# MoE 2 in program order: one queue of weight pieces, pairs and single units in turn, and second products moved into the next unit

## The chip, the cores and the metric

One core of one Trainium2 chip. The metric is the device time of one execution in microseconds (us). Engines: PE (TensorE) multiplies, ACT (ScalarE) copies and applies relu, DVE (VectorE) subtracts, POOL (GpSimd) issues the indirect transfers, SP (SyncE) issues the others.

## The reference

Attention (4 batches, 8 heads, 512 local tokens with a window of 32 to each side, 32 global tokens) gives 2176 rows of 512. Two layers follow:

```
h = x @ w_in                      # 2176x512 @ 512x2048
x = maximum(0.01 * h, h) @ w_out  # MoE 1
logits = normed(x) @ normed(expert_emb).T / tau      # 8 experts
e = argmax(logits); gate = softmax(logits)[e]        # one expert for each token
out = gate * (maximum(x @ w1[e], 0) @ w2[e])         # MoE 2, 512 -> 1024 -> 512
```

All of it is float32. A product is made of three: each operand is split into a high part (rounded to the format PE takes) and a low part (the rest), and PE adds high*high, high*low and low*high.

## The kernel before

The rows are worked on in tiles of 128. Attention is interleaved with MoE 1, which runs over blocks of tiles and, in each, 16 steps of `L1` (first product) and `L2` (second). When 14 of the 17 tiles are done, `make_plan(0)` plans units 0 to 2 of MoE 2; the last three tiles are routed later (`Q0` to `Q4`), and `make_plan(1)`, `make_plan(2)` plan the rest, on DVE, in pieces spread over unit 1.

A **unit** is a group of tokens of one expert. Units 0 to 7 are pairs (two blocks of 128 tokens): eight steps f, each with a first product `D1(u, f)` and, one step later, the second product `D2(u, f)`; between them ACT makes the relu's high part (`g`, L972) and DVE its low part (L973). Units 8 to 13 are singles (one block): `M1(u, j)` for two halves j, relu into `hs` (ACT for j = 0, DVE for j = 1), transposes `HT` on PE into `tp`, `ht` high by ACT (L927) and low by DVE (L928), second product `M2(u, j)`. `ORDER` is the order of the units: 0, 1, 2, 3, 8, 4, 9, 5, 10, 6, 11, 12, 13, 7. More units follow only if the plan needs them.

A unit's weights (4 MB) come by `load_w`, two conditional transfers from SP, into one of two buffers ("lanes": `w1a`, `w2a` and `w1b`, `w2b`); the transfer is skipped where the lane holds that expert already. They are then split in eight **pieces**, a cast on ACT (L863) and a subtraction on DVE (L864) each, for the next unit while this one runs. The tokens' numbers come by `load_ids` (SP, from `idl`, the list that the routing scatters in memory by POOL, L634), their rows by `gather` (POOL, `xg`), and `X2` transposes them (PE L898, ACT `xgT` L899, DVE `xgl` L900). `out_rows` scales (ACT `yo`, L936) and scatters (POOL, L937).

PE and SP run MoE 2 in the order in which the code is written, DVE in units 0 and 1 alone; elsewhere, and on ACT throughout, a scheduler of the framework sets the order. Half of unit 0's pieces are made in the last steps of MoE 1, the others behind its end. At the end of unit 2 the code waits for lane 0 to be free (`load_w(3)`), then loads unit 8 into lane 1, then reads the ids of units 3, 4, 5 and of the singles.

Of the kernel before, what the change touches and what calls it, by code (L numbers as in the profile page):

```python
# [24 lines left out]
def kernel(  # L25
# [519 lines left out]
    def Q0(q, yp):  # L545
# [7 lines left out]
        if NTILE - NL + q == NTILE - 1:  # L553
            x2 = sb.tile([P, XW], F32, tag="xs", bufs=2, name="x2")
# [65 lines left out]
    def Q4():  # L620
# [6 lines left out]
        V.tensor_copy(si, ss[:, 4])  # L627
        V.tensor_reduce(out=ss[:, 5], in_=lg, axis=AX.X, op=ALU.add)
# [107 lines left out]
    def make_plan(phase):  # L736
# [132 lines left out]
    def pieces_w1(u, j):  # L869
        w = w1s[u, j] = sb.tile([P, 2, KM, DM], F32R, tag="half", bufs=8, name="w1s")  # L870
        return split(w, lanes[lane_of[u]][0][:, :, j * DM:(j + 1) * DM])

    def pieces_w2(u, j):
        w = w2s[u, j] = sb.tile([P, 2, 4, DM], F32R, tag="half", bufs=8, name="w2s")
        return split(w, lanes[lane_of[u]][1][:, 4 * j:4 * j + 4, :])
# [29 lines left out]
    def M1(u, j):  # L905
        xT = xts[u]
        w = w1s.pop((u, j))
        hp_ = ps.tile([P, DM], F32, tag="H", name="hp2")
        for a, c in ((0, 0), (1, 0), (0, 1)):
            for k in range(KM):  # L910
                nc.tensor.matmul(
                    hp_, xT[a][:, k, :], w[:, c, k, :], start=(a + c + k == 0), stop=(c == 1 and k == KM - 1)
                )
        hs = sb.tile([P, DM], F32, tag="g", bufs=2, name="hs")
# [27 lines left out]
    def M2(u, j, part):  # L942
        w, ht = w2s[u, j], hts[u, j]
        if j == part == 0:
            ys[u] = ps.tile([P, DM], F32, tag=ybank[u], name="yp2")
        yp = ys[u]
        todo = [(a, c, f) for a, c in ((0, 0), (1, 0), (0, 1)) for f in range(4)]
        for a, c, f in todo[6 * part:6 * part + 6]:
            nc.tensor.matmul(  # L949
                yp, ht[:, a, f, :], w[:, c, f, :], start=(j + a + c + f == 0), stop=(j == c == 1 and f == 3)  # L950
            )
        if part == 0:
            return
        w2s.pop((u, j))
        hts.pop((u, j))
# [4 lines left out]
    def D1(u, f):  # L960
        w = w1s[u, f // 4]
# [7 lines left out]
        if f % 4 == 3:  # L969
            w1s.pop((u, f // 4))  # L970
# [133 lines left out]
    while k < len(steps):  # L1104
        i, f = steps[k]
        if k == KF * (2 * B - 1) + 6:
# [4 lines left out]
            load_w(0)  # L1111
# [33 lines left out]
        if k >= KF * (2 * B - 1) + 10:  # L1145
            if k == KF * (2 * B - 1) + 10:
                lanes[1] = (
                    sb.tile([P, KM, F2], F32, tag="half", bufs=8, name="w1b"),
                    sb.tile([P, KF2, DM], F32, tag="half", bufs=8, name="w2b"),
                )  # L1150
# [3 lines left out]
            first = first[1:]  # L1154
# [26 lines left out]
    def planned(n):  # L1181
        for _ in range(n):
            next(plan_pieces, None)

    pend = []

    def behind():
        if pend:
            pend.pop(0)()

    def unit(k):
# [3 lines left out]
        rest_ = pieces(after) if after is not None else iter(())  # L1195
        same = [m for m in range(k + 1, len(ORDER)) if LANE[m] == LANE[k]]
        if same:
            load_w(ORDER[same[0]])
        if k == NDE - 1:
            load_w(ORDER[LANE.index(1)])  # L1200
# [110 lines left out]
```

## Time and profile before

| | |
|---|---|
| median of 3 runs | 939.44 us (937.65 to 941.67) |
| the profiled execution's own time | 941.09 us |
| its span, first to last instruction | 939.4 us |
| mean granted clock of PE, share of full speed | 0.963 |
| PE busy | 863.3 us, 92% of the span |
| DVE, ACT, POOL busy | 545.5 (58%), 491.5 (52%), 161.1 (17%) |

Own time is what the device takes for the execution; the span is what the profiler saw between its first and last instruction. A busy PE is one with a product under way, at whichever clock.

### The profile page before, as it was taken

Reading aid. Unit: us, or ns where it says so; the run is one execution under the profiler, and the core shown is the slowest. Engines: PE = TensorE matmul, PEld = TensorE weight load, DVE = VectorE, ACT = ScalarE, POOL = GpSimd, SP = SyncE. Lnnn points to the kernel's source line nnn. Section 1 sums busy time; section 2 is a strip of 40 time slices with the busy share of each in tenths; the row PEclk is TensorE's granted clock in tenths of the full one; section 3 lists DMA queues with packets and bytes.
Section 4 is the critical chain, followed back from the end, with each engine's and each line's share of the span. In section 5 each row is a group of like instructions: output and inputs, shape, how many; then the busy total and the mean of one; then the engine's idle time right before and its main releaser. Section 6 shows DMA issues by size and latency. Waiting matters only on the chain.

```text
span 939.4 us, 16083 instructions
## 1 busy us (share of the span) xinstructions
PE 863.3 (92%) x5852; PEld 735.0 (78%) x5852; DVE 545.5 (58%) x1397; ACT 491.5 (52%) x1181; POOL 161.1 (17%) x218
## 2 busy tenths in 40 slices
PE   6768699999999999999999999989796999999996
PEld 3646587888888888888888888978685877878785
DVE  6788898344654554555534345455763566665850
ACT  6877787444645544545423232471452566565841
POOL 3532443001100100000001000210203031220200
PEclk9697899999999999999999999989997999999999
DMA  9676553110121210110000001600157566277600
GB/s 229 168 201 165 148 170 87 44 45 13 36 46 43 54 44 12 46 29 1 12 13 12 12 12 17 220 23 1 45 198 262 202 231 218 87 259 262 229 14 17
DMA packets 104551, 92.21 MB, mean 98 GB/s; under 512 B 73415, under 2 KB 81735, under 8 KB 104466
## 3 DMA queue, kind: packets, MB, share of 16 engines
q1 hardware_dynamic: 98002, 78.51, 27.4%
q0 software_dynamic: 4064, 10.25, 3.4%
q10 hardware_dynamic: 2400, 2.36, 0.8%
q8 instruction: 48, 0.79, 0.4%
q14 instruction: 37, 0.30, 0.1%
HBM read 97.56 MB, written 11.63 MB: 116 GB/s over the span
## 4 chain that ended last, share of the span: by engine, by line
PE 69%; DVE 9%; DMA 8%; issue 6%; ACT 6%; POOL 1%; SPq 1%; POOLq 0%; ACTq 0%; DVEq 0%
PE hps L681 20%; PE yp L703 7%; PE hps L966 7%; PE yp L984 6%; PE yp L705 6%; PE yp L704 6%; DMA out_dram<-yo,ids 2%; DMA ids<-idl 2%; PE av L254 2%; PE pp L240 2%; PE sp L203 2%; PE ga L315 2%; PE yp L949 2%; ACT pr L224 1%; PE lp L505 1%
## 5 line engine op out<-in xcount | busy, mean ns | idle before, releaser
L688 ACT COPY gf<-hps 128x256 f32<-128x256 f32 (+1 forms) x144 | 50.3, 361 | 177.0 <-PE hps L681 176.1
L689 DVE SCALAR_TENSOR_TENSOR gf<-gf 128x256 f32<-128x256 f32 (+1 forms) x144 | 60.0, 425 | 135.6 <-ACT gf L688 135.2
L703 PE MATMUL yp<-woh,g 128*128 128x512 f32 x272 | 114.5, 421 | 0.7 <-ACT g L691 0.7
L984 PE MATMUL yp<-w2s,g 128*128 128x512 f32 x384 | 104.7, 407 | 9.0 <-DVE g L973 6.5
L705 PE MATMUL yp<-woh,g 128*128 128x512 f32 x272 | 107.8, 396 | 1.5 <-DVE g L692 1.5
L704 PE MATMUL yp<-wol,g 128*128 128x512 f32 x272 | 107.5, 395 | 0.0
L984 PEld LDWEIGHTS yp<-w2s,g 128*128 128x128 f32 x384 | 69.1, 194 | 24.6 <-DVE g L973 10.2
L692 DVE TENSOR_TENSOR g<-gf,g 128x256 fp32r<-128x256 f32 (+1 forms) x144 | 60.8, 431 | 42.9 <-ACT g L691 37.4
L966 PE MATMUL hps<-xgT,w1s 128*128 128x256 f32 x512 | 84.3, 288 | 0.0
L966 PEld LDWEIGHTS hps<-xgT,w1s 128*128 128x128 f32 x512 | 75.0, 194 | 4.8
L681 PE MATMUL hps<-xs,wih 128*128 128x256 f32 x448 | 75.6, 291 | 3.2 <-ACT gf L688 3.2
L691 ACT CAST g<-gf 128x256 fp32r<-128x256 f32 (+1 forms) x144 | 55.3, 395 | 34.4 <-DVE gf L689 34.2
L681 PEld LDWEIGHTS hps<-xs,wih 128*128 128x128 f32 x448 | 65.1, 190 | 9.5 <-ACT gf L688 3.4
L681 PE MATMUL hps<-xs,wil 128*128 128x256 f32 x448 | 71.2, 281 | 0.0
L681 PE MATMUL hps<-xl,wih 128*128 128x256 f32 x448 | 71.2, 281 | 0.0
L972 ACT ACTIVATE g<-hps 128x256 fp32r<-128x256 f32 x64 | 24.5, 382 | 86.3 <-PE hps L966 84.3
L705 PEld LDWEIGHTS yp<-woh,g 128*128 128x128 f32 x272 | 51.2, 188 | 14.5 <-DVE g L692 2.4
L703 PEld LDWEIGHTS yp<-woh,g 128*128 128x128 f32 x272 | 51.2, 188 | 12.6 <-issue 4.1
L681 PEld LDWEIGHTS hps<-xs,wil 128*128 128x128 f32 x448 | 60.9, 189 | 0.0
L681 PEld LDWEIGHTS hps<-xl,wih 128*128 128x128 f32 x448 | 60.9, 189 | 0.0
L704 PEld LDWEIGHTS yp<-wol,g 128*128 128x128 f32 x272 | 51.4, 189 | 6.4
L973 DVE SCALAR_TENSOR_TENSOR g<-hps,g 128x256 fp32r<-128x256 f32 x64 | 26.9, 420 | 50.6 <-ACT g L972 50.6
(273 smaller groups left out, 1768.6 us busy)
## 6 DMA issues: line engine op xcount, KB each, us to landing
w1a<-in_moe_w_dram SPq DMA_DIRECT2D x9, 2048.0 KB, 8.4
w2a<-in_moe_w_dram SPq DMA_DIRECT2D x9, 2048.0 KB, 10.8
w1b<-in_moe_w_dram SPq DMA_DIRECT2D x5, 2048.0 KB, 7.8
w2b<-in_moe_w_dram SPq DMA_DIRECT2D x5, 2048.0 KB, 10.1
raw<-in_moe_w_in_dram SPq DMA_DIRECT2D x14, 512.0 KB, 3.7
raw<-in_moe_w_out_dram SPq DMA_DIRECT2D x14, 512.0 KB, 4.6
x2d<-x SPq DMA_DIRECT2D x16, 256.5 KB, 2.8
kn<-in_k_l_dram SPq DMA_DIRECT2D x31, 128.0 KB, 2.8
```

Of the source, the lines that this page charges most:

```text
L681: nc.tensor.matmul(hps, ws[a][:, k], xs[c][k], start=(a + c + k == 0), stop=((a, c) == (1, 0) and k == KM - 1))
L688: nc.scalar.copy(gf, hps[:, cs])
L689: nc.vector.scalar_tensor_tensor(out=gf, in0=gf, scalar=0.01, in1=gf, op0=ALU.mult, op1=ALU.max)
L691: nc.scalar.copy(g[:, 0], gf)
L692: nc.vector.tensor_tensor(out=g[:, 1], in0=gf, in1=g[:, 0].bitcast(F32), op=ALU.subtract)
L703: nc.tensor.matmul(yp, g[:, 0], hi, start=(f == 0), stop=False)
L704: nc.tensor.matmul(yp, g[:, 0], lo, start=False, stop=False)
L705: nc.tensor.matmul(yp, g[:, 1], hi, start=False, stop=(f == KF - 1))
L966: nc.tensor.matmul(hps, w[:, a, k, fs], xts[u][c][:, k], start=(a + c + k == 0), stop=(a == 1 and k == KM - 1))
L972: nc.scalar.activation(out=g[:, 0], in_=hps, func=AF.Relu)
L973: nc.vector.scalar_tensor_tensor(out=g[:, 1], in0=hps, scalar=0.0, in1=g[:, 0].bitcast(F32), op0=ALU.max, op1=ALU.subtract)
L984: nc.tensor.matmul(ys[u, t], g[:, a, t * P:(t + 1) * P], w[:, c, f % 4, :], start=(f + a + c == 0), stop=(f == KF2 - 1 and a == 1),)
```

## The change

MoE 2 is rewritten so that DVE, SP and ACT, beside PE, run it in the order of the code. Pairs use lane 0, singles lane 1; `ORDER` becomes 0, 1, 2, 8, 3, 9, 4, 10, 5, 11, 6, 12, 7, 13. All eight pieces of unit 0 are made in the last six steps of MoE 1. All other pieces stand in one list, `todo`, taken one at each step of units 0 to 2, (2, 2, 1, 2, 1, 2, 1, 1) in a later pair, 2 + 2 in a single; a lane's next load is issued as soon as the lane's last piece is out. The squares of `Q0` become `Q0S` and stand in unit 0's first three steps; the routing and the planning end earlier (`Q4` at step 5 of unit 0, planning from its step 7 to step 3 of unit 1), and `plan_end` follows at step 4 of unit 1, with the weights and the ids of unit 8 first. A single's two second products stand behind the first two steps of the next pair, and a pair's last second product, in two halves, behind the two first products of the single that follows. The numbers of products, pieces and conditional loads are as before (PE has 4 instructions fewer).

```diff
+        rt[q, "x2"] = x2
+
+    def Q0S(q):
         sq = sb.tile([P, DM], F32, tag="x2T", bufs=2, name="sq")
-        nc.scalar.activation(out=sq, in_=x2[:, 0:DM], func=AF.Square, accum_out=lt_["sl3"][:, 0, q:q + 1])
-        rt[q, "x2"] = x2
+        nc.scalar.activation(
+            out=sq, in_=rt[q, "x2"][:, 0:DM], func=AF.Square, accum_out=lt_["sl3"][:, 0, q:q + 1]
+        )
...
-    ORDER = [0, 1, 2, 3, 8, 4, 9, 5, 10, 6, 11, 12, 13, 7]
-    LANE = [0, 0, 0, 0, 1, 0, 1, 0, 1, 0, 1, 0, 1, 0]
-    lane_of = dict(zip(ORDER, LANE))
-    for u in range(ND + NS, NUNIT):
-        lane_of[u] = u % 2
+    ORDER = list(range(NDE))
+    for i in range(max(NS, ND - NDE)):
+        ORDER += ([ND + i] if i < NS else []) + ([NDE + i] if NDE + i < ND else [])
+    lane_of = {u: 0 if u < ND else 1 for u in range(NUNIT)}
...
-    def pieces(u):
-        for j in range(2):
-            for make in (pieces_w1, pieces_w2):
-                for piece in make(u, j):
-                    piece()
-                    yield
+    todo, loaded, live = [], set(), [0]
+    planned = [False]
+
+    def new_pieces(u, late_second):
+        order = [(1, 0), (1, 1), (2, 0), (2, 1)] if late_second else [(1, 0), (2, 0), (1, 1), (2, 1)]
+        return [(u, m, j, i) for m, j in order for i in range(2)]
+
+    for u in ORDER:
+        todo += new_pieces(u, u >= ND)
+
+    def loads():
+        for lane in range(2):
+            rest_ = [u for u in ORDER if lane_of[u] == lane and u not in loaded]
+            if not rest_ or (rest_[0] >= NDE and not planned[0]) or lane not in lanes:
+                continue
+            if any(lane_of[p[0]] == lane and p[0] in loaded for p in todo):
+                continue
+            load_w(rest_[0])
+            loaded.add(rest_[0])
+
+    def piece():
+        if not todo:
+            return None
+        u, m, j, i = todo[0]
+        if u not in loaded or (i == 0 and live[0] == 8 - 2 * (1 in lanes)):
+            return None
+        todo.pop(0)
+        r1, r2 = lanes[lane_of[u]]
+        if m == 1:
+            if i == 0:
+                w1s[u, j] = sb.tile([P, 2, KM, DM], F32R, tag="half", bufs=8, name="w1s")
+            w, src = w1s[u, j], r1[:, :, j * DM:(j + 1) * DM]
+        else:
+            if i == 0:
+                w2s[u, j] = sb.tile([P, 2, 4, DM], F32R, tag="half", bufs=8, name="w2s")
+            w, src = w2s[u, j], r2[:, 4 * j:4 * j + 4, :]
+        live[0] += i == 0
+        ins = split(w, src)[i]()
+        loads()
+        return ins
...
+    def ready(u, m, j, last=1):
+        while any(p[:3] == (u, m, j) and p[3] <= last for p in todo):
+            assert piece() is not None, (u, m, j)
...
-    def D2(u, f):
-        w, g = w2s[u, f // 4], hts.pop((u, f))
-        for t in range(2):
-            if f == 0:
-                ys[u, t] = ps.tile([P, DM], F32, tag=ybank[u], name="yp2")
-            for a, c in ((0, 0), (0, 1), (1, 0)):
-                nc.tensor.matmul(
-                    ys[u, t], g[:, a, t * P:(t + 1) * P], w[:, c, f % 4, :],
-                    start=(f + a + c == 0), stop=(f == KF2 - 1 and a == 1),
-                )
-        if f % 4 == 3:
-            w2s.pop((u, f // 4))
+    def D2(u, f, t):
+        ready(u, 2, f // 4, f % 4 // 2)
+        w, g = w2s[u, f // 4], hts[u, f]
+        if f == 0:
+            ys[u, t] = ps.tile([P, DM], F32, tag=ybank[u], name="yp2")
...
             st(t)
         if k >= KF * (2 * B - 1) + 10:
-            if k == KF * (2 * B - 1) + 10:
-                lanes[1] = (
-                    sb.tile([P, KM, F2], F32, tag="half", bufs=8, name="w1b"),
-                    sb.tile([P, KF2, DM], F32, tag="half", bufs=8, name="w2b"),
-                )
-                first = pieces_w1(0, 0) + pieces_w1(0, 1)
-            for piece in first[:1]:
+            for _ in range((2, 1, 1, 2, 1, 1)[k - KF * (2 * B - 1) - 10]):
...
-    for t in range(2):
-        X2(0, t)
-    L2(*state["prev"])
-    for t in range(NL):
-        with tc.high_priority(offset=0):
-            Q0(t, ys.pop((2 * B - 1, t)))
-    for piece in pieces_w2(0, 0) + pieces_w2(0, 1):
...
+    def plan_end():
+        planned[0] = True
+        lanes[1] = (
+            sb.tile([P, KM, F2], F32, tag="half", bufs=8, name="w1b"),
+            sb.tile([P, KF2, DM], F32, tag="half", bufs=8, name="w2b"),
+        )
+        loads()
+        for u in ORDER[NDE:NDE + 3]:
+            load_ids(u)
...
 
         def x2(t):
             if after is not None and t < len(cols_of(after)):
@@ -1213,68 +1240,72 @@
             for fn, a in due.get((k, f), []):
                 fn(*a)
 
+        def fetch():
+            if k + 2 < len(ORDER) and k >= NDE - 1:
+                if k + 3 < len(ORDER) and k >= NDE:
+                    load_ids(ORDER[k + 3])
+                gather(ORDER[k + 2])
+
         if u < ND:
+            count = (1,) * KF2 if k < NDE else (2, 2, 1, 2, 1, 2, 1, 1)
             for f in range(KF2):
                 D1(u, f)
-                behind()
+                behind(1 if f == 0 and ORDER[k - 1] >= ND else len(pend))
                 due_at(f)
-                next(rest_, None)
-                if f >= 5:
+                some(count[f])
+                if f == 1:
+                    fetch()
+                if f in (5, 6):
                     x2(f - 5)
-                if k == 0 and f == 4:
-                    gather(ORDER[2])
-                pend.append(lambda f=f: D2(u, f))
+                pend.append(lambda f=f: D2(u, f, 0))
+                pend.append(lambda f=f: D2(u, f, 1))
             return
         M1(u, 0)
         behind()
-        for _ in range(2):
-            next(rest_, None)
+        x2(0)
         HT(u, 0)
-        x2(0)
+        some(2)
         M1(u, 1)
-        for _ in range(2):
-            next(rest_, None)
-        M2(u, 0, 0)
+        fetch()
+        behind()
         x2(1)
+        if after is None:
+            M2(u, 0)
         HT(u, 1)
-        M2(u, 0, 1)
-        for _ in range(4):
-            next(rest_, None)
-
-        def last():
-            M2(u, 1, 0)
-            M2(u, 1, 1)
-
-        pend.append(last)
+        some(2)
+        pend.extend([lambda j=j: M2(u, j) for j in range(after is None, 2)])
 
     due = {
-        (0, 0): [(Q1, (0,)), (Q1, (1,))], (0, 1): [(Q1L, (0,)), (Q1L, (1,)), (Q1, (2,))], (0, 2): [(Q1L, (2,))],
-        (0, 3): [(Q2, ())], (0, 5): [(Q3, ())], (0, 6): [(Q4, ())],
-        (1, 0): [(planned, (2,))], (1, 1): [(planned, (2,))], (1, 2): [(planned, (2,))], (1, 3): [(planned, (2,))],
+        (0, 0): [(Q1, (0,)), (Q1, (1,)), (Q0S, (0,))], (0, 1): [(Q1L, (0,)), (Q1L, (1,)), (Q1, (2,)), (Q0S, (1,))],
+        (0, 2): [(Q1L, (2,)), (Q0S, (2,))], (0, 3): [(Q2, ())], (0, 4): [(Q3, ())], (0, 5): [(Q4, ())],
+        (0, 7): [(plan_on, (1,))], (1, 0): [(plan_on, (2,))], (1, 1): [(plan_on, (2,))], (1, 2): [(plan_on, (2,))],
+        (1, 3): [(plan_on, (3,))], (1, 4): [(plan_end, ())], (1, 6): [(gather, (ORDER[NDE],))],
     }
-    with tc.manual_schedule(engines={mybir.EngineType.DVE, mybir.EngineType.SP}):
-        for k in range(2):
+    with tc.manual_schedule(engines={mybir.EngineType.DVE, mybir.EngineType.SP, mybir.EngineType.Activation}):
+        for t in range(2):
+            X2(0, t)
+        L2(*state["prev"])
+        for t in range(NL):
+            Q0(t, ys.pop((2 * B - 1, t)))
+        gather(ORDER[2])
+        for k in range(len(ORDER)):
             unit(k)
-    with tc.manual_schedule(engines={mybir.EngineType.SP}):
-        for k in range(2, len(ORDER)):
-            unit(k)
-        behind()
+        behind(len(pend))
```

ACT at the start of unit 0, just behind the squares of the last tiles. Before (`w1s` and `w2s` are split weights, `g` the relu of a step):

```order
L863 CAST w2s<-w2a 128x1024 x4
L972 ACTIVATE g_7297<-hps_7284 128x256
L863 CAST w1s<-w1a 128x1024 x2
L972 ACTIVATE g_7330<-hps_7317 128x256
L863 CAST w2s<-w2a 128x1024 x2
L863 CAST w1s<-w1a 128x1024 x2
L863 CAST w2s<-w2a 128x1024 x2
L972 ACTIVATE g_7372<-hps_7359 128x256
```

Now, behind the copies of the last tiles (`sq` are their squares):

```order
L1009 ACTIVATE g_7297<-hps_7284 128x256
L562 ACTIVATE sq,sl_7264<-x_7270 128x512
L865 CAST w1s<-w1a 128x1024
L1009 ACTIVATE g_7332<-hps_7319 128x256
L562 ACTIVATE sq,sl_7264<-x_7272 128x512
L865 CAST w1s<-w1a 128x1024
L1009 ACTIVATE g_7376<-hps_7363 128x256
L562 ACTIVATE sq,sl_7264<-x_7274 128x512
L865 CAST w2s<-w2a 128x1024
```

Four casts ahead of the first relu and eight ahead of the third are gone; a square and one cast stand ahead of each.

SP where the plan is complete. Before, in unit 2 (`ids` are the tokens' numbers):

```order
L847 DMA w1a<-in_moe_w_dram 128x4x1024
L848 ISA
L848 DMA w2a<-in_moe_w_dram 128x8x512
L845 TENSOR_LOAD plan
L845 ISA x2
L846 TENSOR_LOAD plan
L846 ISA x2
L847 ISA
L847 DMA w1b<-in_moe_w_dram 128x4x1024
L848 ISA
L848 DMA w2b<-in_moe_w_dram 128x8x512
L840 TENSOR_LOAD plan
```

Now, in unit 1:

```order
L849 DMA w1b<-in_moe_w_dram 128x4x1024
L850 ISA
L850 DMA w2b<-in_moe_w_dram 128x8x512
L842 TENSOR_LOAD plan
L842 ISA x2
L843 REGISTER_ALU
L843 DMA ids<-idl 128x1
```

The ids follow the loads of lane 1 in both; the loads of lane 0 for unit 3, which stood ahead, stand four reads of ids later.

DVE in a single, from the relu's transposed half on (`xgl` is the low part of the next pair's tokens, `hs` the single's second relu). Now:

```order
L936 TENSOR_TENSOR xgl_8237<-xgp,xgT 128x4x128
L966 TENSOR_TENSOR ht<-tp,ht 128x512
L866 TENSOR_TENSOR w1s<-w1a,w1s 128x1024 x2
L956 TENSOR_SCALAR hs<-hp_8260 128x512
L936 TENSOR_TENSOR xgl_8237<-xgp,xgT 128x4x128
L966 TENSOR_TENSOR ht<-tp,ht 128x512
L866 TENSOR_TENSOR w2s<-w2a,w2s 128x1024 x2
```

Before, the same place of a single:

```order
L864 TENSOR_TENSOR w1s<-w1a,w1s 128x1024 x2
L864 TENSOR_TENSOR w2s<-w2a,w2s 128x1024 x2
L864 TENSOR_TENSOR w1s<-w1a,w1s 128x1024
L918 TENSOR_SCALAR hs<-hp_8571 128x512
L864 TENSOR_TENSOR w1s<-w1a,w1s 128x1024
L928 TENSOR_TENSOR ht<-tp,ht 128x512
L900 TENSOR_TENSOR xgl_8561<-xgp,xgT 128x4x128
```

The second `hs` stood behind one piece of its pair of pieces and now stands behind both.

## Rows read from the trace of the kernel before

**Rows 1.** Windows by stage (units 0, 1, 2, the rest, the tail): length, busy times, PEclk
```profile
620.71:657.12 36.41, 31.44 (x193) 28.11 (x191) 19.26 (x39) 17.61 (x31) 3.00 (x5) 0.86 0.06 15
657.12:688.75 31.63, 26.20 (x153) 22.20 (x152) 24.77 (x82) 13.07 (x20) 6.12 (x5) 0.95 0.11 34
688.75:723.91 35.16, 26.04 (x153) 23.12 (x152) 14.63 (x19) 13.88 (x21) 9.03 (x13) 0.85 0.83 300
723.91:930.57 206.66, 198.02 (x1119) 167.43 (x1117) 128.95 (x152) 118.23 (x169) 36.26 (x38) 0.99 0.48 172
930.57:939.40 8.83, 0.00 (x0) 0.00 (x0) 0.00 (x0) 0.76 (x2) 1.94 (x2) 0.77 0.12 42
```

**Rows 2.** PE's waits, 560 to 940: total, times, longest
```profile
PE xgp L898 <- DMA xg<-x2d,ids: 9.1, 1, 9.1
PE yp L984 <- DVE g L973: 6.5, 5, 2.5
PE yp L949 <- ACT ht L927: 4.1, 4, 1.0
PE yp L949 <- DVE ht L928: 3.9, 4, 1.0
```

**Rows 3.** Chain of work: a pair's first and second product
```profile
766.82 1.41 PE hps L966 x12
768.23 1.40 PE yp L984 x6
```

**Rows 4.** Timeline, start of unit 0: ACT, PE
```profile
622.94 3.88 ACT L863 CAST w2s<-w2a 128x1024 fp32r<-128x1024 f32 x4
627.15 0.74 PE L984 MATMUL yp<-w2s,g 128*128 128x512 f32 x2 [2.57 <-ACT g L972]
```

**Rows 5.** Windows (columns of rows 1): MoE 1's end, then stretches behind waits
```profile
600.00:620.00 20.00, 20.00 (x104) 17.87 (x103) 10.53 (x25) 9.62 (x24) 6.30 (x9) 1.00 0.19 53
...
624.50:640.00 15.50, 11.79 (x52) 10.59 (x51) 10.51 (x13) 10.81 (x14) 1.49 (x1) 0.67 0.00 0
668.97:672.50 3.53, 3.53 (x13) 3.15 (x14) 3.10 (x22) 3.53 (x5) 0.45 (x1) 0.52 0.01 0
714.98:720.66 5.68, 5.68 (x23) 5.16 (x23) 1.12 (x2) 0.97 (x2) 1.67 (x5) 0.54 0.92 321
755.90:762.40 6.50, 5.45 (x20) 4.37 (x21) 6.34 (x8) 3.58 (x6) 3.83 (x4) 0.74 0.74 269
...
798.59:799.38 0.79, 0.79 (x10) 0.79 (x8) 0.79 (x1) 0.16 (x1) 0.79 (x1) 1.00 0.00 0
```

**Rows 6.** Sum over six windows that hold the planning pieces of DVE
```profile
sum 8.68, PE 8.42 PEld 7.52 DVE 7.66 ACT 4.33 POOL 2.16; mean PE 1.40 PEld 1.25 DVE 1.28 ACT 0.72 POOL 0.36
```

**Rows 7.** From routing to gather: POOL's scatters (timeline), then the chain of work
```profile
657.05 1.07 POOL L634 DMA_INDIRECT idl<-tok,si  x1 [31.05 <-DVE sl L629]
...
676.06 1.90 POOL L634 DMA_INDIRECT idl<-tok,si  x1 [6.64 <-DMA idl<-tok,si]
...
693.41 13.39 DMA ids<-idl
...
707.85 6.99 DMA xg<-x2d,ids
```

**Rows 8.** Groups by line from 620 on: busy us, mean ns
```profile
L973 DVE SCALAR_TENSOR_TENSOR g<-hps,g 128x256 fp32r<-128x256 f32 x64 | 26.9, 420 | 50.6 <-ACT g L972 50.6
...
L936 ACT ACTIVATE yo<-yp,gate 128x512 f32<-128x512 f32 x22 | 14.7, 689 | 12.3 <-issue 7.0 <-PE yp L984 2.8 <-PE yp L949 2.4
...
L918 DVE TENSOR_SCALAR hs<-hp 128x512 f32<-128x512 f32 x6 | 4.1, 682 | 0.0
```

**Rows 9.** Timeline: two pieces, cast by ACT and subtracted by DVE
```profile
692.40 1.98 ACT L863 CAST w1s<-w1a 128x1024 fp32r<-128x1024 f32 x2
...
693.47 2.36 DVE L864 TENSOR_TENSOR w1s<-w1a,w1s 128x1024 fp32r<-128x1024 f32 x2 [2.27 <-ACT w1s L863]
```

**Rows 10.** Timeline of POOL at the end
```profile
934.42 0.97 POOL L937 DMA_INDIRECT out_dram<-yo,ids  x1 [2.53 <-ACTq L1263]
```

More of the change, by code (lines that the diff above doesn't have):

```diff
@@ L553, in Q0 @@
         if NTILE - NL + q == NTILE - 1:
-            x2 = sb.tile([P, XW], F32, tag="xs", bufs=2, name="x2")
+            x2 = late["pool"].tile([P, XW], F32, tag="xw", bufs=2, name="x2")
         else:
@@ L867, in split, with used_up @@
         return [lambda c=slice(i, i + 2): piece(c) for i in (0, 2)]
[L869 to L875, printed above, removed]
[L877 to L882 removed]
+    todo, loaded, live = [], set(), [0]
[37 more added lines that the diff above has]
+            assert piece() is not None, (u, m, j)
+    def used_up(ws, key):
+        ws.pop(key)
+        live[0] -= 1
     def X2(u, t=0):
@@ L940, in out_rows, with M2 @@
         )
-    def M2(u, j, part):
-        w, ht = w2s[u, j], hts[u, j]
-        if j == part == 0:
+    def M2(u, j):
+        ready(u, 2, j)
+        w, ht = w2s[u, j], hts.pop((u, j))
+        if j == 0:
             ys[u] = ps.tile([P, DM], F32, tag=ybank[u], name="yp2")
         yp = ys[u]
-        todo = [(a, c, f) for a, c in ((0, 0), (1, 0), (0, 1)) for f in range(4)]
-        for a, c, f in todo[6 * part:6 * part + 6]:
-            nc.tensor.matmul(
-                yp, ht[:, a, f, :], w[:, c, f, :], start=(j + a + c + f == 0), stop=(j == c == 1 and f == 3)
-            )
[L952 to L955, printed above, removed]
+        for a, c in ((0, 0), (1, 0), (0, 1)):
+            for f in range(4):
+                nc.tensor.matmul(
+                    yp, ht[:, a, f, :], w[:, c, f, :], start=(j + a + c + f == 0), stop=(j == c == 1 and f == 3)
+                )
+        used_up(w2s, (u, j))
         if j == 1:
@@ L960, in D1 @@
     def D1(u, f):
+        ready(u, 1, f // 4)
         w = w1s[u, f // 4]
@@ L1179, with plan_on, behind, some @@
     plan_pieces = late_plan()
-    def planned(n):
+    def plan_on(n):
         for _ in range(n):
             next(plan_pieces, None)
-    pend = []
-    def behind():
-        if pend:
-            pend.pop(0)()
+    def plan_end():
[3 more added lines that the diff above has]
+            sb.tile([P, KF2, DM], F32, tag="half", bufs=8, name="w2b"),
+        )
+        loads()
+        for u in ORDER[NDE:NDE + 3]:
+            load_ids(u)
+    pend = []
+    def behind(n=1):
+        for _ in range(n):
+            if pend:
+                pend.pop(0)()
+    def some(n):
+        for _ in range(n):
+            piece()
     def unit(k):
@@ L1194, in unit @@
         after = ORDER[k + 1] if k + 1 < len(ORDER) else None
[L1195 to L1200, printed above, removed]
-        for m in {NDE - 1: (NDE, NDE + 1, NDE + 2)}.get(k, (k + 3,) if k >= NDE else ()):
-            if m < len(ORDER):
-                load_ids(ORDER[m])
-        for m in {0: (2,), NDE - 1: (NDE, NDE + 1)}.get(k, (k + 2,) if k >= NDE else ()):
-            if m < len(ORDER) and k:
-                gather(ORDER[m])
+        single = after is not None and after >= ND
         def x2(t):
@@ L1266 @@
             load_w(u)
+            loaded.add(u)
             load_ids(u)
@@ L1269 @@
             X2(u)
-            for _ in pieces(u):
-                pass
+            todo.extend(new_pieces(u, True))
             for j in range(2):
```

32 lines of the change are left out of this document (18 added, 14 removed).

## The prediction

> **What bounds the kernel now.** I read the stage windows first [rows 1]. PE is busy 92% of the span, and in units 3 to 7 with the singles it is busy 198.02 of 206.66 us at a granted clock of 0.99: no rearrangement takes much there. The three units ahead of them are worse: 36.41, 31.63 and 35.16 us, where a pair's eight steps cost 8 x (1.41 + 1.40) = 22.5 us of products [rows 3]. PE stands idle for 4.97 us in unit 0, 5.43 in unit 1, 9.12 in unit 2 and 8.64 in the rest (length less PE busy), 28.2 in all. Behind the last product 8.83 us go by without PE.
>
> Then the list of PE's waits [rows 2], for what ends these: 9.1 us once for the gathered tokens of unit 3; 6.5 in five waits for the low part of `g` on DVE; 4.1 and 3.9 at the four singles that have a wait for `ht`, about 2 us for each such single. Unit 0 adds 2.57 us for the high part of `g` on ACT, which stands behind four casts of 3.88 us [rows 4].
>
> Last the clock. Behind some of the waits PE works at a mean granted clock between its levels of 1.2 and 2.4 GHz [rows 5]: 0.67 over 15.50 us of unit 0, 0.52 over 3.53 of unit 1, 0.54 over 5.68 behind the gather, 0.74 over 6.50 in the first single. One minus the clock times the length gives 5.1 + 1.7 + 2.6 + 1.7 = 11.1 us, an upper estimate, as some of that time is idle.
>
> So some 39 us beyond the products lie in MoE 2, and 8.83 in the tail. The change touches all of these places and takes no product away. I sum what is removed and what appears.
>
> **Unit 0.** The four pieces that stood behind MoE 1 move into its last six steps. They cost four casts and four subtractions, some 4 + 5 us, there; in the last 20 us of MoE 1 PE is busy throughout, while ACT works 9.62 and DVE 10.53 us [rows 5], so they are hidden. Without that cover they would cost what they do now. What appears is a square: it reuses the buffer of a transposed tile, so ACT waits for that tile's routing product, and the next cast and the relu of step 1 stand behind it; DVE has a subtraction before the low part of that relu. I estimate 1.0 us of wait on PE; below it is nothing (routing and step 2 could cover it), above it the 3.7 us that the unit has now (2.57 and one of the waits for DVE).
>
> **Unit 1.** The planning now stands in DVE's order in steps 0 to 2 nearly whole. Its pieces take 8.68 us [rows 6]. With four low parts of 0.42 [rows 8] and three subtractions of 1.18 [rows 9], DVE has 13.9 us of work from the low part of step 0 to that of step 3, and begins about 0.4 us after the first product. PE has in that time four steps of 2.81 and the 0.5 us of the high part of step 3: 11.7. The difference, 2.6 us, is the stall, at steps 2 and 3; I take 2.5. Before, unit 1 waited 5.43. Its bounds are 0.9 (if DVE's queue is empty longer ahead) and those 5.4.
>
> **The gather of the first late unit.** In the trace, the three routing scatters start at 657.05 and, the last, at 676.06, each behind the landing of the one before [rows 7]; ids of units 3 to 5 and 8 are read only from 693.41 on, since SP stands first at lane 0 and then issues lane 1's weights, and the first lands 13.39 us later behind those 4 MB; the gather takes 6.99 more. Now the routing ends a step earlier in a shorter unit 0, some 16 us sooner: its first scatter goes at about 641, the last, with the same gaps, at about 660 and has landed by 671. `plan_end` in step 4 of unit 1 has by then issued w1b and w2b at about 664. The ids of unit 8 are read at 671 at the latest, land by 684 even if all of 13.39 us counts again, and are gathered by 691.5 with 6.99 us. PE wants them in step 5 of unit 2, which begins at about 620.7 + 27.3 + 27.0 = 675 (the windows of now less the waits and the clock above), so at 690 to 691. So the 9.1 us vanish, with a margin of 0 in the worst case and 7 to 9 us if the ids need little beside transfers of weights that are part done. I take nothing; the upper bound is the 9.1 that it costs now.
>
> **Singles.** Second products now run later, in the next pair, and `ht` is no longer waited for. In their place the second `hs` stands on DVE behind two subtractions. Let the first product M1(u, 0) of a single end at T. ACT has then `hs`, `yo`, `xgT` and `ht`, at most four times 0.69 [rows 8], then two casts; the subtractions end 695.83 - 692.40 = 3.43 us after the first cast began [rows 9]; `hs` takes 0.68 [rows 8]: T + 6.9. PE has two halves of a second product at 0.70, M1(u, 1) at 2 x 1.40 (12 products of 512 columns) [rows 3] and three groups of transposes at 0.40 (two take 0.79) [rows 5]: T + 5.4. So a wait of 1.5 us before the second `HT` in each of singles 8 to 12, 7.5 us. Single 13 has no pieces left to make; its last `ht` costs about 1.0. The bounds are nothing (DVE takes the subtractions sooner) and 2.0 for each.
>
> A rule of the Trainium skill bears on this ("TensorE: Matmul & The Clock Gate", section "A second HAM failure mode: psum-queue depth-cycling"): in a kernel that changes PSUM banks, frequent short idle times between groups of products made the clock swing between its levels, and the time went on going down and up again. The trace agrees for one single only, whose clock fell to 0.74 [rows 5]. By the rule, singles would go as in the first rival below.
>
> **Tail.** The order ends with a single, so one block is scaled and scattered instead of two. The second scatter of now was issued at 934.42 and the span ends 4.98 later [rows 10]; before it go one `yo` of 0.69 and about 0.1 of start. That is 5.8 to 5.9 us instead of 8.83, 2.9 less.
>
> **The sum,** against the profiled span of 939.4: less 28.2 of idle time, plus 1.0 + 2.5 + 7.5 + 1.0 = 12.0 of new waits, less 11.1 of clock, plus 3.4 for the clock after the waits that stay (one such as unit 1's, 1.7, and one such as the first single's, 1.7), less 2.9: 912.6. Time outside the span is 1.69 us (941.09 - 939.40), and the profiled execution lies 1.65 above the median of 939.44, so the span's sum stands for the median as it is. I give **912**. Clock terms are bounded by 0 and 11.1.
>
> **The rivals.**
> 1. *The clock falls in every single.* Then the other four singles lose 1.7 us each as the first one does now: 912.6 + 6.8 = **919**. For it: the wait of 1.5 in one piece is longer than each of the two of 1.0 now. Against it: of four singles with the same two waits, one fell.
> 2. *The gather of unit 8 is as late as that of unit 3 was.* The full 9.1 of wait, and 2.6 of clock behind it: 912.6 + 11.7 = **924**. For it: the ids are still issued behind 4 MB of weights, and 0.83 of the DMA engines' time was taken in unit 2 [rows 1]. Against it: both start 20 us or more sooner.
> 3. *The singles do not wait,* because ACT's casts start sooner than in my list: 912.6 - 7.5 - 1.7 = **903**.
> 4. *ACT stands at weights that have not landed (slower than before).* In program order a cast whose load is late holds the relu behind it, and PE with it; a scheduler's order is no longer there to move it. Eleven loads are fresh from unit 8 on. A lane is reloaded when its last piece is out, and its next piece comes at the shortest after six steps of a pair and one first product of a single: 6 x 2.81 + 2.8 = 19.7 us. The ids behind two loads landed after 13.39 [rows 7], so there are 6 us to spare. From 2.4 us late for each load the whole gain of 26.8 is gone; to be over 0.5% slower, 944, needs 2.9 each, that is, landing after 22.6 us: **945** or more.
> 5. *No effect:* the stalls return elsewhere in full, 939.
>
> **How the numbers follow.** Forecast 0.58 (907 to 917: unit 0, unit 1 and singles within half of their bounds), rival 1 0.15, rival 2 0.12, rival 3 0.09, rival 4 0.04, no effect 0.02. The range reaches from rival 3, 902, past rival 2 to 927, since the upper bounds of units 0 and 1 add 2.7 and 2.9. A change of 0.5%, 4.7 us, is about what a measurement of this kernel can tell from none. Only rival 4 is slower, only no effect is the same; all else is faster: 0.94, 0.02, 0.04.
>
> **What would show it.** Unit 0's window should be some 27 us long and unit 1's 27, with clocks above 0.9; the wait for `xg` should be gone from the list; no wait for `ht` in singles 8 to 12, and one of 1.2 to 1.8 us for `hs` on DVE in each, behind the two subtractions; the tail should be below 6 us. I am wrong if PE waits for `xg` of unit 8, if relus on ACT wait for weights, if the last steps of MoE 1 become longer than they are, or if a clock below 0.8 stands in several singles.

## The result and the profile after

The changed kernel takes 906.48 us (median of 4 runs, 906.35 to 908.00) against 940.56 (4 runs, 937.65 to 944.16) for the kernel before: a ratio of 0.964, 95% interval 0.9603 to 0.9676. Forecast were 912 us and a range of 902 to 927. One of the six executions of a later run (the second relu of a single on ACT) took 2062.25 us, for no reason that the record shows, and the ratio of that run leaves it out.

Windows of the changed kernel in the stages of [rows 1] (length, busy times, PEclk; unit 2 now ends where single 8 begins, and the tail begins, as in [rows 1], where the last product ends), with the end of MoE 1 ahead of them:

```profile
600.00:619.66 19.66, 19.66 (x102) 17.59 (x101) 13.52 (x25) 12.20 (x26) 5.94 (x9) 1.00 0.19 54
619.66:646.50 26.84, 26.72 (x192) 24.09 (x191) 17.55 (x45) 14.13 (x27) 3.71 (x5) 1.00 0.34 49
646.50:672.47 25.97, 23.94 (x154) 20.93 (x152) 21.70 (x72) 13.01 (x21) 4.25 (x4) 1.00 0.38 41
672.47:696.97 24.50, 23.63 (x150) 20.84 (x149) 13.45 (x18) 12.54 (x20) 7.84 (x11) 1.00 0.82 301
696.97:896.82 199.85, 194.55 (x1122) 167.11 (x1121) 131.49 (x154) 119.13 (x170) 37.06 (x42) 1.00 0.54 190
896.82:904.60 7.78, 0.00 (x1) 0.00 (x0) 0.00 (x0) 0.69 (x1) 0.97 (x1) 0.69 0.09 32
```

Spans go from 939.4 to 904.6, 34.8 us. Stage by stage, measured and (in brackets) what the prediction's terms come to: the stretch ahead of unit 0, 1.05 (0); unit 0, 9.6 (9.1); unit 1, 5.7 (2.9); unit 2, 10.7 (11.7); the rest, 6.8 (0.1); the tail, 1.1 (2.9). At the end of MoE 1, where unit 0's pieces now stand, PE is busy throughout.

PE's waits in the changed kernel, in all, times, longest; against [rows 2] the gather's 9.1 us and nearly all waits for `ht` are gone, and a wait for `hs` is new:

```profile
PE tp L963 <- DVE hs L956: 4.6, 5, 0.9
PE yp L1021 <- DVE g L1010: 2.5, 2, 2.0
PE yp L988 <- ACT ht L965: 0.7, 1, 0.7
PE yp L1021 <- ACT g L1009: 0.3, 1, 0.3
```

The first single (timelines of ACT, DVE and PE) shows where that wait comes from:

```profile
699.81 0.60 ACT L954 ACTIVATE hs<-hp 128x512 f32<-128x512 f32 x1 [2.88 <-PE hp L948]
...
702.08 2.02 ACT L865 CAST w1s<-w1a 128x1024 fp32r<-128x1024 f32 x2
...
703.18 2.36 DVE L866 TENSOR_TENSOR w1s<-w1a,w1s 128x1024 fp32r<-128x1024 f32 x2
705.46 0.68 DVE L956 TENSOR_SCALAR hs<-hp 128x512 f32<-128x512 f32 x1
...
706.20 0.66 PE L963 MATMUL tp<-ident,hs 128*128 128x128 f32 x4 [0.93 <-DVE hs L956]
```

Two subtractions stand ahead of `hs`, as forecast; the casts begin 2.3 us after the first relu may start, where four copies of 0.69 gave 2.8. The other waits are the one in step 3 of unit 1 (1.96 us, forecast 2.5 for the unit), two in unit 2 of 0.29 and 0.58 behind the first cast of `w1b`, and the last `ht`.

The gather, on POOL's timeline: the last of the three scatters and the first of the four gathers behind it, the one for unit 8.

```profile
660.36 0.96 POOL L639 DMA_INDIRECT idl<-tok,si  x1 [6.72 <-DMA idl<-tok,si]
...
684.93 1.05 POOL L855 DMA_INDIRECT xg<-x2d,ids  x1 [4.88 <-DMA ids<-idl]
```

The rows landed 4.4 us behind this issue, at 689.4, and PE took them up at 690.74 with no wait in the list: a margin of 1.4 us. With [rows 7]'s 7.0 us for the transfer they would have landed at 691.9, 1.2 us late.

### The profile page after: what moved, and what is told of

The parts are those of the page before. It is cut to its first block, busy times and chain, and to the rows that moved or that the text cites. A ratio compares the mean times of both kernels' runs of the same rounds, so it can differ in the third digit from the quotient of the medians.

```text
span 904.6 us, 16057 instructions
## 1 busy us (share of the span) xinstructions
PE 848.2 (94%) x5852; PEld 724.7 (80%) x5852; DVE 547.1 (60%) x1397; ACT 491.2 (54%) x1181; POOL 158.4 (18%) x218
## 4 chain that ended last, share of the span: by engine, by line
PE 74%; DVE 8%; DMA 7%; issue 5%; ACT 4%; SPq 1%; POOL 0%; POOLq 0%; ACTq 0%; DVEq 0%
PE hps L686 21%; PE yp L708 7%; PE hps L1003 7%; PE yp L710 7%; PE yp L709 7%; PE yp L1021 6%; PE av L254 3%; PE sp L203 3%; PE pp L240 3%; PE yp L988 2%; DMA out_dram<-yo,ids 2%; DMA w1b<-in_moe_w_dram 2%; PE hp L948 2%; PE ga L315 2%; ACT pr L224 1%
## 5 line engine op out<-in xcount | busy, mean ns | idle before, releaser
L1021 PE MATMUL yp<-w2s,g 128*128 128x512 f32 x384 | 102.2, 396 | 3.0 <-DVE g L1010 2.5
L1003 PEld LDWEIGHTS hps<-xgT,w1s 128*128 128x128 f32 x512 | 72.3, 188 | 4.2
L696 ACT CAST g<-gf 128x256 fp32r<-128x256 f32 (+1 forms) x144 | 55.3, 395 | 34.9 <-DVE gf L694 34.8
L866 DVE TENSOR_TENSOR w2s<-w2a,w2s 128x1024 fp32r<-128x1024 f32 x32 | 38.3, 1222 | 21.1 <-ACT w2s L865 21.1
```

What stands on the lines that cost most here:

```text
L696: nc.scalar.copy(g[:, 0], gf)
L866: nc.vector.tensor_tensor(out=w[:, 1, c], in0=src[:, c], in1=w[:, 0, c].bitcast(F32), op=ALU.subtract)
L1003: nc.tensor.matmul(hps, w[:, a, k, fs], xts[u][c][:, k], start=(a + c + k == 0), stop=(a == 1 and k == KM - 1))
L1021: nc.tensor.matmul(ys[u, t], g[:, a, t * P:(t + 1) * P], w[:, c, f % 4, :], start=(f + a + c == 0), stop=(f == KF2 - 1 and a == 1),)
```

## Experiments

Each edit is against the changed kernel unless said otherwise. The stretch ahead of unit 0 varies by some us between profiles though its code is the same, so parts are compared as "MoE 2": from unit 0's first product to the end. That is 318.7 us before, 284.9 in the changed kernel and 283.0 in a second profile of it (the last run below). Ratios are to the kernel before.

**Unit 0's last four pieces late**

```diff
-            for _ in range((2, 1, 1, 2, 1, 1)[k - KF * (2 * B - 1) - 10]):
+            for _ in range((1, 1, 1, 1, 0, 0)[k - KF * (2 * B - 1) - 10]):
...
             Q0(t, ys.pop((2 * B - 1, t)))
+        for _ in range(4):
+            piece()
```

> The changed kernel, but with the last four of unit 0's eight pieces behind the copies of the last tiles, as before the change, in place of the last steps of MoE 1. Theory: the four casts (3.9 us) stand ahead of the first relu of unit 0, PE waits at least 2.5 us for it and its clock falls behind that wait as it did before; unit 0's window goes from 26.8 to 32 to 36 us, the time to 912 to 916. Rival (the casts are cheap by themselves, and the clock fell for another reason): only the wait of 2.5 to 3.7 us, clock 1.00, time 909 to 910.

910.2 us (908.80 to 914.17), ratio 0.9678 (0.9651 to 0.9706); MoE 2 290.7, unit 0 32.3. PE's timeline, then windows behind it:

```profile
626.58 0.73 PE L1021 MATMUL yp<-w2s,g 128*128 128x512 f32 x2 [1.04 <-ACT g L1009]
628.46 1.20 PE L1021 MATMUL yp<-w2s,g 128*128 128x512 f32 x4 [1.15 <-DVE g L1010]
```

```profile
630.00:635.00 5.00, 5.00 (x26) 5.00 (x27) 2.78 (x4) 3.48 (x7) 0.00 (x0) 0.53 0.00 0
635.00:640.00 5.00, 5.00 (x31) 4.53 (x30) 2.16 (x3) 1.93 (x4) 0.89 (x1) 0.78 0.00 0
```

The wait is 2.2 us, and the clock behind it gives another 0.47 x 5 + 0.22 x 5 = 3.5: 5.7 of the 5.8 us. In this execution the clock in unit 0 did hang on the casts, as the theory says. But it is the slowest of the five, 914.17 us; the median lies 3.7 us above the changed kernel, below the 912 to 916 of the theory and next to the rival's 909 to 910. How much clock the other executions lost is not shown.

**ACT left to the scheduler**

```diff
-    with tc.manual_schedule(engines={mybir.EngineType.DVE, mybir.EngineType.SP, mybir.EngineType.Activation}):
+    with tc.manual_schedule(engines={mybir.EngineType.DVE, mybir.EngineType.SP}):
```

> The changed kernel, but ACT's order is left to the framework's scheduler; the orders of PE, DVE and SP are the same to the row. The scheduler puts casts in blocks again, six of them between the relus of steps 1 and 2 of unit 0. Theory that ACT's program order is what keeps relus in time: PE waits 3 to 6 us for relu high parts in unit 0, some more in units 1 and 2, and the clock falls there; time 912 to 920. Rival that the new places of the pieces do it and ACT's order matters little: 905 to 908.

932.28 us, ratio 0.992 (0.9891 to 0.9948): far beyond what was expected. PE and DVE have the same order to the row, so of the 34 us gained 26 go when ACT's order alone goes. PE's waits, and windows of unit 1's end, the first single and the next pair and single:

```profile
PE tp L963 <- DVE hs L956: 11.6, 5, 2.3
PE hps L1003 <- ACT xgT L935: 4.6, 5, 0.9
```

```profile
665.00:670.00 5.00, 5.00 (x22) 4.44 (x23) 3.16 (x6) 2.37 (x3) 0.31 (x1) 0.66 0.77 70
700.00:720.00 20.00, 16.76 (x74) 13.78 (x73) 11.87 (x14) 12.12 (x17) 7.24 (x8) 0.83 0.52 171
720.00:760.00 40.00, 36.77 (x209) 31.50 (x209) 22.91 (x29) 23.25 (x33) 8.41 (x9) 0.97 0.70 243
```

I had looked for the loss in unit 0; 22.5 of the 25.3 us that MoE 2 is longer lie behind the start of the first single (222.4 us to the last product at a clock of 0.95, for 199.9 at 1.00). ACT's timeline there:

```profile
704.31 0.60 ACT L954 ACTIVATE hs<-hp 128x512 f32<-128x512 f32 x1 [1.94 <-PE hp L948]
704.80 1.98 ACT L865 CAST w2s<-w2a 128x1024 fp32r<-128x1024 f32 x2
706.68 0.69 ACT L974 ACTIVATE yo<-yp,gate 128x512 f32<-128x512 f32 x1
707.27 0.58 ACT L935 CAST xgT<-xgp 128x512 fp32r<-128x512 f32 x1
707.73 0.61 ACT L965 CAST ht<-tp 128x512 fp32r<-128x512 f32 x1
```

The scheduler takes two casts of `w2s`, wanted much later, ahead of `yo`, `xgT` and `ht`; DVE, in program order, waits for these with `hs` behind it. Each single then waits 2.3 + 0.9 us, and the clock falls behind it: the first rival's mechanism, with a cause that the changed kernel does not have.

The list has no wait for `ht` in singles 8 to 12: only the last, of 0.7 us, is there, as in the changed kernel. The second products are in their new places here, so these places keep the waits for `ht` away without ACT's order: DVE has the first half of `ht` ready at 709.2, and its product, in the next pair, begins at 716.4.

**ACT's order alone, on the kernel before**

```diff
-    with tc.manual_schedule(engines={mybir.EngineType.DVE, mybir.EngineType.SP}):
+    with tc.manual_schedule(engines={mybir.EngineType.DVE, mybir.EngineType.SP, mybir.EngineType.Activation}):
         for k in range(2):
             unit(k)
-    with tc.manual_schedule(engines={mybir.EngineType.SP}):
+    with tc.manual_schedule(engines={mybir.EngineType.SP, mybir.EngineType.Activation}):
```

> The kernel before the change, with one part of the change alone: ACT too runs MoE 2 in the order of the code; the orders of PE and SP are the same to the row. Theory that program order on ACT pays only with the pieces put where the relus leave room: the wait behind four casts in unit 0, the gather's 9.1 us and the waits for ht in singles stay, and the waits for DVE become a little shorter; 930 to 940. Rival that ACT's order by itself carries most of the gain (leaving it to the scheduler cost 25 us in the changed kernel): 912 to 925.

928.83 us, ratio 0.990 (0.9879 to 0.9922), MoE 2 306.7. That is 1.2 us below the theory's range and 3.8 above the rival's. PE's waits:

```profile
PE xgp L898 <- DMA xg<-x2d,ids: 9.2, 1, 9.2
PE yp L984 <- ACT g L972: 3.5, 2, 2.6
PE yp L984 <- DVE g L973: 2.7, 4, 0.9
PE hps L966 <- DVE xgl L900: 2.5, 5, 1.4
PE yp L949 <- DVE ht L928: 0.3, 2, 0.2
```

The casts of unit 0 and the gather cost what they did, but the waits for `ht` fell from 8.0 us to 0.3 although no second product was moved. The theory had them stay. The waits for the low part of `g` fell as well, from 6.5 to 2.7. ACT between the two relus of the first single, on the kernel before and then in this run:

```profile
750.41 1.98 ACT L863 CAST w2s<-w2a 128x1024 fp32r<-128x1024 f32 x2
...
753.45 2.00 ACT L863 CAST w1s<-w1a 128x1024 fp32r<-128x1024 f32 x2
755.33 0.60 ACT L927 CAST ht<-tp 128x512 fp32r<-128x512 f32 x1
```

```profile
744.93 1.99 ACT L863 CAST w1s<-w1a 128x1024 fp32r<-128x1024 f32 x2
746.81 0.58 ACT L927 CAST ht<-tp 128x512 fp32r<-128x512 f32 x1
```

Two casts of `w2s` no longer stand ahead of `ht`. DVE's order changed too, as the scheduler sets it from unit 2 on: in the first single its `ht` now stands ahead of the second `hs` (748.3 and 748.9) and stood behind it (757.4 and 755.7). So the edit is of ACT, but of those 8.0 us the 3.9 that ended with DVE's low part of `ht` are not parted from DVE's own order.

**M2(u, 0) back in the single**

```diff
         M1(u, 0)
-        behind()
-        x2(0)
+        behind(len(pend))
         HT(u, 0)
+        x2(0)
...
-        behind()
+        M2(u, 0)
         x2(1)
```

> The changed kernel, but a single's first second product M2(u, 0) stands in the single, behind M1(u, 1) and ahead of HT(u, 1), as before the change, and the pair's last second product stands whole behind M1(u, 0); only M2(u, 1) stays in the next pair. Theory that moving these products is what took the waits for ht away: M2(u, 0) gives the second hs time, so its wait of 0.93 goes, and waits for ht of about 1 us (high or low half) come in its place, two in each single; MoE 2 becomes 3 to 6 us longer, time 909 to 913. Rival that the place of M2(u, 0) matters little: within 1.5 us, 905 to 908.

904.72 us, ratio 0.9636 (0.9612 to 0.9661), not to be told from the changed kernel by time; MoE 2 281.8. The waits tell:

```profile
PE yp L1021 <- DVE g L1010: 2.0, 1, 2.0
PE hps L1003 <- ACT xgT L935: 1.2, 5, 0.2
PE yp L988 <- ACT ht L965: 0.7, 1, 0.7
```

`hs` is no longer waited for, and no wait for `ht` comes in its place: 3.9 us of waits in all instead of 8.1. The theory is right on `hs` and wrong on `ht`: with ACT in program order the singles need no moved product to be free of waits for `ht`. Taking M2(u, 0) out of them opened the wait for `hs`: of the edit's parts only this one puts more products, twelve, ahead of the second `HT`.

**Second relu of a single on ACT**

```diff
-        if j == 0:
-            nc.scalar.activation(out=hs, in_=hp_, func=AF.Relu)
-        else:
-            nc.vector.tensor_scalar(out=hs, in0=hp_, scalar1=0.0, scalar2=None, op0=ALU.max)
+        nc.scalar.activation(out=hs, in_=hp_, func=AF.Relu)
```

> The changed kernel, but the second relu of a single is made by ACT instead of by DVE, where it stood behind two subtractions. Theory that the waits of 0.93 us in each of five singles come from those subtractions: the waits for hs (4.6 us in all) go or fall below 0.3 us each, and at most half of it comes back as waits for the next pair's tokens, whose copy stands behind the relu on ACT; time 902 to 905. Rival that PE would wait there anyway (for ACT's casts ahead of the relu): the wait is the same or longer, 906 to 910.

904.65 us, ratio 0.9624 (0.960 to 0.9648), MoE 2 282.5. The waits for `hs` are gone, and five of 0.43 us for `xgT` stand in their place (2.1 in all): the theory, though the time alone does not separate it from the changed kernel.

**Routing and planning one step later**

```diff
-        (0, 2): [(Q1L, (2,)), (Q0S, (2,))], (0, 3): [(Q2, ())], (0, 4): [(Q3, ())], (0, 5): [(Q4, ())],
-        (0, 7): [(plan_on, (1,))], (1, 0): [(plan_on, (2,))], (1, 1): [(plan_on, (2,))], (1, 2): [(plan_on, (2,))],
-        (1, 3): [(plan_on, (3,))], (1, 4): [(plan_end, ())], (1, 6): [(gather, (ORDER[NDE],))],
+        (0, 2): [(Q1L, (2,)), (Q0S, (2,))], (0, 3): [(Q2, ())], (0, 5): [(Q3, ())], (0, 6): [(Q4, ())],
+        (1, 0): [(plan_on, (2,))], (1, 1): [(plan_on, (2,))], (1, 2): [(plan_on, (2,))],
+        (1, 3): [(plan_on, (2,))], (1, 4): [(plan_on, (2,))], (1, 5): [(plan_end, ())], (1, 7): [(gather, (ORDER[NDE],))],
```

> The changed kernel, but the last routing steps stand one step of unit 0 later and the planning one step later, plan_end at step 5 of unit 1 and the gather of unit 8 at step 7. In the changed kernel the ids of unit 8 landed and the gather went out at 684.9, and PE took up the gathered rows at 690.7 without a listed wait. Theory that the margin is about nothing: the gather comes 2.8 to 3.3 us later, and PE waits 2 to 4 us for xg in unit 2; time 908 to 911. Rival of a margin of 7 to 9 us: no wait for xg, 905 to 908.

911.01 us, ratio 0.9688 (0.9661 to 0.9716). PE's timeline in unit 2:

```profile
694.98 0.63 PE L934 MATMUL xgp<-ident,xg 128*128 128x128 f32 x4 [3.48 <-DMA xg<-x2d,ids]
```

The wait of the theory is there, but its sum is not the theory's. The gather went out at 686.29, only 1.4 us later than in the changed kernel, and its rows landed 8.5 us behind it in place of 4.4. With 4.4 the rows would have come before PE wanted them, at 691.5. So the longer transfer makes the wait, and the step of delay by itself would not have. Why the transfer takes longer is not shown.

**Ids ahead of the weights**

```diff
-        loads()
         for u in ORDER[NDE:NDE + 3]:
             load_ids(u)
+        loads()
```

> The changed kernel, but plan_end reads the four columns of ids first and issues the loads of lane 1 (w1b, w2b of unit 8) behind them. In the changed kernel w1b was issued at 663.6, landed at 678.6, and ACT's first cast of it started then, with 0.29 and 0.58 us of wait on PE; the four ids took SP 9.56 us from 668.6 on, as they wait for the scattered list. Theory that in program order a late load stops ACT and with it the relus (rival 4 of the prediction): w1b is issued near 678, lands near 687 to 690, the relu behind its first cast comes 8 to 11 us late, PE waits that long in unit 2 and its clock falls behind it; time 915 to 921. The ids land earlier and the gather goes out before 680. Rival that the margin of the loads covers it: 905 to 908.

913.27 us, ratio 0.9725 (0.9707 to 0.9743). SP's timeline, and PE's where the relu is late:

```profile
670.58 3.63 SPq L843 DMA_DIRECT2D ids<-idl  x4
675.71 0.38 SPq L849 DMA_DIRECT2D w1b<-in_moe_w_dram  x1
```

```profile
688.17 3.39 PE L1021 MATMUL yp<-w2s,g 128*128 128x512 f32 x6 [5.82 <-ACT g L1009]
```

The wait for late weights is there, on ACT's relu, and the six products behind it take 3.39 us instead of 1.40 to 1.57. It is 5.8 us and not 8 to 11, since the four ids took 3.6 us without weights ahead of them, not 9.6. The gather went out at 675.1, as expected before 680. The fourth rival's mechanism is real; the changed kernel meets it in one load only, for 0.87 us.

**Four repairs together**: both relus on ACT as above; in a single `x2(1)` ahead of `behind()`; and

```diff
-            count = (1,) * KF2 if k < NDE else (2, 2, 1, 2, 1, 2, 1, 1)
+            count = ((1,) * KF2, (1, 0, 0, 0, 1, 1, 2, 2), (1, 0, 2, 1, 1, 1, 1, 2))[k] if k < NDE else (2, 2, 1, 2, 1, 2, 1, 1)
...
-                    x2(f - 5)
+                    x2(f - 5 - single)
```

> The changed kernel with four repairs: both relus of a single on ACT; in a single the transposes of the next pair's second block ahead of the copy of the pair's output; unit 1 makes pieces in steps 0 and 4 to 7 (1, 0, 0, 0, 1, 1, 2, 2) so that the planning has DVE for itself, unit 2 makes nine (1, 0, 2, 1, 1, 1, 1, 2); the tokens of a single are transposed one step later, at step 6. Theory that each remaining wait is what its releaser says: the 1.96 us in unit 1, the 0.87 in unit 2 and the 4.6 in singles all but vanish, MoE 2 goes from 284.9 to 277 to 280 us, time 898 to 902. Rival that the gather, which had no margin, takes it back, as unit 2 now starts 2 us sooner: a wait for xg of 1 to 3 us, time 901 to 904.

903.99 us, ratio 0.963 (0.9612 to 0.9647), MoE 2 281.4. PE's waits:

```profile
PE xgp L934 <- DMA xg<-x2d,ids: 3.4, 1, 3.4
PE yp L985 <- ACT ht L962: 0.7, 1, 0.7
```

All the small waits went as their releasers said, and the rival came true all the same: the gather took 3.4 us back. It went out at 684.26, 0.7 us sooner than in the changed kernel, and PE wanted the rows at 689.1, 1.7 us sooner; but they landed 8.1 us behind the issue, where they took 4.4 in the changed kernel. With 4.4 they would have been in time here too: as with the routing one step later, the longer transfer makes the wait.

**Ids of unit 8 between the two loads**, on top of that:

```diff
+        if between is not None:
+            load_ids(between)
         nc.sync.dma_start(w2r, w2[bass.ds(e, 1)].rearrange("o (k p) f -> p (o k) f", p=P), cond=cond)
...
-        loads()
-        for u in ORDER[NDE:NDE + 3]:
+        u = ORDER[NDE]
+        load_w(u, between=u)
+        loaded.add(u)
+        loads()
+        for u in ORDER[NDE + 1:NDE + 3]:
             load_ids(u)
```

> The combined kernel of the run before, with one edit on SP: at the end of the planning the ids of unit 8 are read between the two weight loads of lane 1 (w1b, ids of 8, w2b, the other ids). In the combined kernel the first gather went out at 684 behind 4 MB of weights and PE waited 3.42 us for its rows. Theory that the ids stood behind the weights in the transfers' queue: with 2 MB ahead of them the gather goes out 4 to 7 us earlier, the wait for xg goes, w2b is late by nothing (its first piece is four steps behind that of w1b), and MoE 2 goes from 281.4 to 276 to 278 us; time 897 to 900. Rival that the scattered list, not the weights, is what the ids wait for: the gather stays at 682 to 684, the wait at 2 to 3.4 us, time 901 to 905.

898.5 us (896.82 to 901.72), ratio 0.956 (0.9534 to 0.9587), MoE 2 276.7. SP's and POOL's timelines, PE's only wait, and a window from unit 0's first product to 1.1 us behind the last:

```profile
668.30 0.36 SPq L843 DMA_DIRECT2D ids<-idl  x1
669.02 0.42 SPq L852 DMA_DIRECT2D w2b<-in_moe_w_dram  x1
```

```profile
677.43 1.05 POOL L857 DMA_INDIRECT xg<-x2d,ids  x1 [0.30 <-issue]
```

```profile
PE yp L987 <- ACT ht L964: 0.7, 1, 0.7
```

```profile
619.79:890.00 270.21, 268.24 (x1614) 233.23 (x1612) 180.38 (x281) 163.10 (x243) 56.77 (x61) 1.00 0.55 177
```

With 2 MB ahead of the ids the gather goes out at 677.4, 9.1 us behind their issue; with 4 MB it was 17 (667.2 to 684.3 in the combined kernel), and with none 4.6 (670.6 to 675.1 in the run with ids ahead of weights). The weights in the queue were what the ids waited for. This version beats both kernels.

**The changed kernel again**, without an edit, on the same chip:

> The changed kernel itself once more, beside the run with ids between the loads on the same chip: 905 to 908, and a span of MoE 2, from unit 0's first product to the end, within 1 us of 284.9. The stretch ahead of unit 0 varied from 616.9 to 621.7 us between the profiles so far with the same code there, so parts are compared from unit 0's first product on.

905.98 us, ratio 0.9662 (0.9627 to 0.9698); MoE 2 283.0, 1.9 shorter than in the first profile, where 1 us was expected: a difference in MoE 2 below 2 us between two runs shows nothing. The first single's wait is 0.93 again and unit 1's 1.97, but the 0.87 us in unit 2 are absent: `w1b` was in time in this execution. The first gather took 4.3 us, with a margin of 1.2.

## Why the prediction was right

It was right in direction and its range held; the time came out 5.5 us below the forecast, just below the band of 907 to 917 that had the chance of 0.58. The spans differ from it by 8.0 us, and that splits as follows: 1.05 ahead of unit 0, 0.5 in unit 0, 2.7 in unit 1, 6.7 in the rest, less 1.1 in unit 2 and 1.9 in the tail.

- **Unit 0** (1.0 us of new wait, 5.1 of clock given back): measured, no wait in the list and a clock of 1.00, 9.6 us for 9.1. The profile with late pieces, of the slowest of five executions, gives 5.8 of these back, and shows that wait and clock go together there.
- **Unit 1** (a stall of 2.5 us of DVE's backlog): 1.96. The 1.7 us of clock that I kept for it were not lost; that is most of the 2.7 us by which the term was off.
- **The gather** (9.1 us gone): right, and in part by luck. The ids and the gather came when forecast (684.93 for 684), but the margin of 1.4 us comes from a transfer of 4.4 us where the prediction had 6.99. With its own 6.99 PE would have waited 1.2 us, and with the 8.1 and 8.5 of two later runs 2.3 to 2.7. In the second profile the transfer took 4.3 us. Unit 2 came out 1.1 us worse than forecast, mostly by the 0.87 us for `w1b`.
- **Singles** (five waits of 1.5, one of 1.0, one fall of the clock): the mis-sized term. The mechanism was right, two subtractions ahead of `hs`, but a wait is 0.93: I priced four ACT copies by the slowest of them, 0.69, where the casts began after 2.3 us. With the last wait at 0.7 us for 1.0, that is 3.2 of the 6.7 us. The rest is busy time of PE, 194.55 us for 198.02: 3.5 us less, where the sum had given back 1.7 us of clock and taken as much away again. The clock did not fall, which is 1.7 of these; the other 1.8 no run explains.
- **Why the old waits went** is where the account was incomplete. The prediction had: "Second products now run later, in the next pair, and `ht` is no longer waited for." That is enough, as the run with ACT left to the scheduler shows, which has the moved products and no such waits. But it is not needed: the kernel before with ACT in program order lost those waits without moving a product, and the run with M2(u, 0) back in its place did not get them back. The moved product also made the new wait for `hs`. ACT's order was listed only as a danger (rival 4); taking it out of the changed kernel costs 26 of the 34 us, and putting it into the one before, where DVE's order changes with it, gives 10.
- **The tail** (2.9 less): 8.83 to 7.78, 1.05 less, not the 5.8 to 5.9 us of the forecast. The prediction took the time behind the second scatter of before, 4.98 us, for that of the only one of now. The scatter of now went out at 897.87, 6.73 us ahead of the span's end, and landed 4.0 us behind its issue, where the second of before took 2.3. In the nine other profiles of kernels with this ending 6.35 to 8.24 us go by behind the last product. Why the landing takes longer is not shown.
- **Rivals.** A clock that falls in every single: not in the changed kernel, where five waits of 0.93 us left the clock at 1.00, but in the run with ACT left to the scheduler, with 2.3 and 0.9 us in each single. The Trainium skill describes a clock that swings between its levels where short idle times between groups of products are frequent ("TensorE: Matmul & The Clock Gate", section "A second HAM failure mode: psum-queue depth-cycling"). The first of these traces does not show it, the second agrees. A late gather: a longer transfer away. Late weights: shown by ids ahead of weights, at 5.8 us for one load.

Still open: the 1.05 us ahead of unit 0. The first product of unit 0 lay between 616.9 and 622.3 us in all profiles after the change, with pieces in the same places in most, so it is not a gain that one profile can show.

## What to carry to other kernels

Where one engine's queue feeds another that runs in a fixed order, fix its order too: work that is not urgent, placed by a scheduler ahead of a short copy, is paid in waits on the engine behind, and again in its clock. Put a small transfer that a chain waits for ahead of the large one behind which it would queue, and split the large one if it is wanted soon as well. Before tightening a stage, look for the transfer that has little margin left: it can take the gain back.

## What the runs showed of the hardware

The clock behind a wait did not follow the wait's length alone. One wait of 1.96 us in unit 1 left it at 1.00 in the changed kernel; one of 2.02 at the same step in the run with ACT left to the scheduler, with one of 0.77 some 3 us ahead of it, was followed by a mean of 0.66 over 5 us; two of 1.04 and 1.15, 0.7 us apart, were followed by 0.53. What sets it between these cases, the runs do not tell.

The gather of unit 8's rows landed 4.1 to 8.5 us behind its issue, in kernels that differ little: 4.1 to 4.4 in four profiles, 6.3 and 6.9 in two, 8.1 and 8.5 in two. A margin that is taken from one profile of such a transfer need not hold for the next.
